# An attention and two MLP layers in one kernel: small VectorE steps on GpSimd, 1/rms stored as rows, an earlier load of the fourth chunk, and 128x128 transposes

## The chip, the cores and the metric

The kernel runs on one core of a Trainium2 chip. A core has TensorE (matrix products and transposes, results in PSUM), VectorE, ScalarE, GpSimd and a queue SP that issues DMAs; all of them run side by side, each works through its own instructions in order, and they wait for each other through semaphores. The metric is the device time of one execution in microseconds (us): 1201.92 us, the median of three runs (1201.45 to 1202.34).

## The reference

```
# q, k, v: [4 batches, 8 heads, 576, 64]
scores = q @ k.T / sqrt(64)
thresh = max(scores, row) - tau                 # tau = 0.02
scores = where(scores >= thresh, scores, -1e9) - max(row)
attn   = exp(scores); attn = attn / (sum(attn, row) + 1e-9)
x      = (attn @ v), heads side by side         # [2304 tokens, 512]

rms = sqrt(mean(x*x, row) + 1e-6)               # first MLP, d_ff 1536
xn  = x / rms * rms_g
x   = (silu(xn @ w_gate) * (xn @ w_val)) @ w_out

h   = x @ w_in                                  # second MLP, d_ff 2048
out = (h * cos(h)) @ w_out2
```

## The kernel before

**Three stages, one stream.** The attention handles 16 pairs of heads (4 batches x 4 pairs). Of each pair, tokens 0 to 511 are four units of 128 rows per head, and the last 64 rows of both heads make a fifth unit (`q4`, `k4`, `v4` hold these rests). The two MLPs work on six chunks of 384 tokens; the first in 6 groups of 2 tiles of d_ff, the second in groups of 3 or 2. In both MLPs every product is three multiplications (`mm3`, L694) of halves: a value is split into a rounded `hi` and a rest `lo`.

**A pair in the attention.** `load_k`, `load_q`, `load_v` issue the DMAs. `prep_pe` transposes q and k on TensorE in three steps a, b, c, and `prep_act` copies them out of PSUM (q scaled by -1/sqrt(64)). The rest of k (64 rows of both heads) is transposed in b and once more in c as a 64-row operand (`k4_t`, L414); the rest of q is scaled by `scale_q4` (VectorE, L417). Then, per unit: `s_mm` (TensorE, L475) makes negated scores for both heads; `s_max` (VectorE, L496) copies them out of PSUM and takes their minimum m; `s_exp` (ScalarE, L514) makes exp(m - s); `s_thr` (VectorE, L505) adds tau to the m of a group of units (two, two, and the last one); `s_mask` (VectorE, L524) multiplies by s <= threshold and sums the row. `t_pe` and `c_pe` transpose the masked exponentials on TensorE, `t_raw` and `c_raw` copy them back, `av` multiplies by v (L599), and `av_out` copies the result. `r_inv` adds 1e-9 to the sums and takes the reciprocal (L533, L534), transposes blocks of 32x32 (L535), `r_out` and `r_in` carry the result through DRAM to one row over all partitions, and `av_div` multiplies (GpSimd, L616). `x_out` stores the pair's x in DRAM.

**The norm.** GpSimd squares and adds the pairs of a batch (`x_sq`, `x_add`), TensorE sums over partitions (`x_sum`), VectorE scales (`x_mean`, L644), GpSimd takes the power -0.5 (`rms`, L648), and two DMAs store 1/rms in DRAM (`rms_out`, L652 and L653): the result lies down the partitions, so each element is stored on its own. A chunk's x is loaded from DRAM, 1/rms of its tokens is loaded to all partitions, GpSimd multiplies, and ScalarE and VectorE split it into `xh` and `xl`.

**What sets the order.** In the attention `Plan` writes the order of all engines: each step has an engine, a cost in ns and a place (`STEPS`), and a greedy loop always takes the step that can start first by these costs; ties go by place. PSUM, loaded tiles and exponentials are counted as buffers. The chunks 0, 1 and 2 and the first four gate-and-value steps of the first MLP (`gv`, TensorE pgv) are in this order too. Behind it stands a plain loop: per step a product with w_out of an earlier step (`o1`, px), the next gate-and-value step, its SiLU and split, and `pump`, which advances weight loads and conversions (up to three at once). In that loop, before the change: the chunks 3 and 4 are loaded ahead of the first turn, chunk 5 two chunks ahead; one chunk ahead GpSimd scales `acc` by 1/rms in one step (L1046) and `split_x` makes the halves (L684, L688). When a chunk's two products with w_out are done, VectorE copies or adds four tiles out of PSUM into `acc` (L1006). The memory of the attention is released before the loop and used again for weights, `acc` and halves.

Of the kernel before, what the change touches and what calls it, by code (L numbers as in the profile page):

```python
# [18 lines left out]
P = 128  # L19
# [9 lines left out]
    "none": ("", 0, 41153),  # L29
    "load_k": ("SP", 1700, -139209, 5000),  # L30
    "load_q": ("SP", 1700, -7544, 7000),
    "load_v": ("SP", 1700, 15881, 5000),
    "q4": ("DVE", 200, -12635),
    "pb": ("PE", 450, -19772),
    "pa": ("PE", 450, -32518),
    "pc": ("PE", 560, -19721),
    "pb_a": ("ACT", 550, 114770),
    "pa_a": ("ACT", 690, -200654),
    "pc_a": ("ACT", 440, -28030),
    "s": ("PE", 1150, -34045),  # L40
    "s4": ("PE", 1050, 22554),
    "warm": ("PE", 640, 119554),
    "max": ("DVE", 830, -156788),
    "exp": ("ACT", 785, 24918),
    "th": ("DVE", 90, 31050),
    "mask": ("DVE", 960, 9378),
    "t": ("PE", 445, 37058),
    "raw": ("ACT", 595, 4406),
    "c0": ("PE", 220, 28723),
    "c1": ("PE", 440, 25563),  # L50
    "c_raw": ("ACT", 415, 126770),
    "rinv": ("DVE", 400, -7759),
    "r_out": ("SP", 2100, 50027, 2500),
    "r_in": ("SP", 1700, 14486, 5000),
    "av0": ("PE", 2300, -173062),
    "av1": ("PE", 2850, -137138),
    "avo": ("ACT", 420, 11229),
    "div": ("POOL", 1420, 191515),
    "xout": ("SP", 500, -109300, 2500),
    "sq": ("POOL", 1200, -50998),  # L60
    "x_add": ("POOL", 1420, 62249),
    "xsum": ("PE", 1150, 65176),
    "mean": ("DVE", 150, -247496),
    "rms": ("POOL", 1330, 44384),
    "rs_out": ("SP", 1000, 78246, 9000),
    "x_load": ("SP", 500, 173724, 6000),
    "x_p": ("POOL", 1000, 66803),
    "x_a": ("ACT", 610, 106078),
    "x_d": ("DVE", 610, 40293),
    "jdma": ("SP", 500, 85880, 5000),  # L70
    "j1": ("DVE", 600, 330),
    "j2": ("DVE", 690, -17065),
    "j_p": ("POOL", 2500, 43119),
    "j_a": ("ACT", 620, 46809),
    "gv": ("PE", 2100, 50075),
    "silu": ("ACT", 500, -103082),
    "hmul": ("DVE", 560, -12918),
    "hhi": ("ACT", 520, 149881),
    "hlo": ("DVE", 720, -101475),
}  # L80
SIGNAL = 100
WARM = (8, 2, 0, 0)
# [10 lines left out]
class Plan:  # L93
# [19 lines left out]
    def order(self):  # L113
# [14 lines left out]
        out = []  # L128
        while len(out) < len(steps):
            best = None  # L130
            for eng, ns in here.items():
                for n in list(ns):
                    s = steps[n]
                    held = [taken[tag][-self.bufs[tag]] for tag, _ in s["take"]
                            if len(taken[tag]) >= self.bufs[tag]]
                    wait = [key for key in held if users.get(key, 1)]
                    if wait:
                        parked.setdefault(wait[0], []).append(n)
                        ns.remove(n)
                        continue  # L140
                    t = max([ready[n], clock[eng]] + [freed[key] for key in held])
                    if best is None or (t, s["place"], n) < best:
                        best = t, s["place"], n
# [3 lines left out]
            eng = s["eng"]  # L147
            here[eng].remove(n)
# [27 lines left out]
def attention_moe_cos_kernel(  # L176
# [27 lines left out]
    IDLE1 = 6  # L204
    G2 = (3, 3, 3, 3, 2, 2)
# [148 lines left out]
    r32 = [acst.tile([P, 32], F32, name=f"r32{i}") for i in range(4)]  # L354
# [58 lines left out]
    def k4_t(ps, p):  # L413
        nc.tensor.transpose(ps, nat["k", p][1].rearrange("p h d -> p (h d)"), ident[:64, :64])  # L414

    def scale_q4(p):
        nc.vector.tensor_scalar(q4[p % 2], q4[p % 2], qscale[:, 0:1], None, op0=ALU.mult)  # L417

    def prep_pe(p, kind):
# [6 lines left out]
        elif kind == "b":  # L426
            k4_t(ps[:, 0:64], p)
            nat_t(ps[:, 64:512], nat["k", p][0], range(3))
        else:
            nat_t(ps, nat["k", p][0], (3,))  # L430
            k4_t(ps[:, 128:192], p)
            nc.tensor.transpose(ps[:, 192:320], q4[p % 2], ident)

    PREP_COLS = {"a": (0, 512), "b": (0, 448), "c": (448, 768)}

    def prep_act(p, kind):
        nm = "q" if kind == "a" else "k"
        if (nm, p) not in qk:
            w = 512 if kind == "a" else S + 192
# [24 lines left out]
    def s_mm(n):  # L464
# [5 lines left out]
        for c in range(2):  # L470
            for hd in heads(n):
                k0 = 288 * c + (0 if hd else 64)
                r = slice(0, P) if u == 4 else slice(64 * hd, 64 * hd + 64)
                lhs = kh[:, S + 64:] if u == 4 else qk["q", p][r, u * P:(u + 1) * P]
# [53 lines left out]

    def r_inv(p):
# [3 lines left out]
        nc.vector.tensor_scalar(r[:, :9], pr[p]["sum"], 1.0e-9, None, op0=ALU.add)  # L533
# [107 lines left out]
    def x_mean(b):  # L641
        ps = sq.pop(("ps", b))
        rm[b] = sm_p.tile([P, 5], F32, tag="rm", name="rm")
        nc.vector.tensor_scalar(rm[b], ps[:, 0:5], 1.0 / DM, 1.0e-6, op0=ALU.mult, op1=ALU.add)  # L644

    def rms(b):

        nc.gpsimd.tensor_tensor(rm[b], rm[b], expo, op=ALU.pow)  # L648

    def rms_out(b):  # L650
        r = rs_dram[b * S:(b + 1) * S]
        nc.sync.dma_start(r[0:512].rearrange("(t p) -> p t", p=P), rm[b][:, 0:4])  # L652
        nc.sync.dma_start(r[512:S], rm[b][64:P, 4:5])  # L653
# [56 lines left out]
    def h_tiles(n):  # L710
        w, t = ((S + 192, "k"), (512, "q"))[n % 2]
# [21 lines left out]
    def gv_h(n):  # L733
        for fn in (h_silu, h_mul, h_hi, h_lo):
            fn(n)

    def attention():
# [84 lines left out]
        for j in range(2 * NPAIRS):  # L822
# [16 lines left out]
            if par:  # L839
                x = add("rinv", n1, r_inv, p, after=[mk[n, hd] for n in range(5 * p, 5 * p + 5) for hd in heads(n)])  # L840
# [8 lines left out]
            if par:  # L849
# [10 lines left out]
                if hp == NP - 1:  # L860
# [4 lines left out]
                    x = add("rms", n1, rms, b, after=[x])  # L865
                    done["rs", b] = add("rs_out", n1, rms_out, b, after=[x])
# [51 lines left out]
        def grow_2():  # L918
            att_s.close()
            late[2] = ctx.enter_context(tc.tile_pool(name="xhl2", bufs=1, side="right"))  # L920

# [19 lines left out]
        )  # L941
        hs = []
# [12 lines left out]
    with tc.manual_schedule():  # L955
# [11 lines left out]
        acc_p = ctx.enter_context(tc.tile_pool(name="acc", bufs=NCH))  # L967
        t_rs = ctx.enter_context(tc.tile_pool(name="rs", bufs=2))
        late.update({c: x_p for c in range(3, NCH)})

# [5 lines left out]

        def load_x(c):
            xrs[c] = t_rs.tile([P, TC], F32, tag="rs", name="rs")
            nc.sync.dma_start(xrs[c], rs_dram[c * TC:(c + 1) * TC].partition_broadcast(P))
            acc[c] = acc_p.tile([P, KD, TC], F32, tag="acc", name="acc")  # L980
            nc.sync.dma_start(acc[c], x_dram[:, :, c * TC:(c + 1) * TC])
# [4 lines left out]
        def o1(n):  # L986
# [13 lines left out]
            if i == fs[-1]:  # L1000
                if c not in acc:
                    acc[c] = acc_p.tile([P, KD, TC], F32, tag="acc", name="acc")
# [22 lines left out]
        load_x(3)  # L1025
        load_x(4)
# [10 lines left out]

        for n in range(N_EARLY, len(seq)):
# [4 lines left out]
            if g == 0 and 4 < c + 2 < NCH and i == fs[0]:  # L1043
                load_x(c + 2)
            if g == 0 and 3 <= c + 1 < NCH and i == fs[0]:
                nc.gpsimd.tensor_tensor(  # L1046
                    acc[c + 1], acc[c + 1],
                    xrs[c + 1][:, None, :].broadcast_to([P, KD, TC]), op=ALU.mult,
                )
# [11 lines left out]
        m1.close()  # L1061

# [143 lines left out]
```

## Time and profile before

| | |
|---|---|
| median of three runs | 1201.92 us |
| the profiled execution, its span | 1201.75 us, 1200.0 us |
| TensorE, busy | 1169.6 us (97%) |
| VectorE, busy | 886.9 us (74%) |
| ScalarE, busy | 648.5 us (54%) |
| GpSimd, busy | 380.1 us (32%) |
| mean granted clock of TensorE | 0.995 of full speed |

The span runs from the first to the last instruction; PE is TensorE's multiplications, PEld its loading of weights, DVE VectorE, ACT ScalarE, POOL GpSimd, SPq the queue of DMA issues. Busy shares are means over stages with different limits, so they are read by stretches: the attention runs to about 334 us, the first MLP to about 770 us, the second to the end.

### The profile page before, as it was taken

The page shows a single profiled execution, that of the slowest core. Times are in us where ns is not written, and L with a number is a line of the kernel's source. Part 1 is how long each engine was busy: PE and PEld are TensorE (multiplying, and loading weights), DVE is VectorE, ACT ScalarE, POOL GpSimd, SP SyncE. Part 2 cuts the span into 40 slices and gives each one's busy share as a digit, 9 for nine tenths or more (in the row PEclk, how much of TensorE's full clock was granted, in tenths as well). Part 3 has the DMA queues.
Part 4 walks back from the last instruction along what each step waited for, and adds up shares of the span by engine and source line. Part 5 has one row for each costly group of instructions (what it writes and reads, how often), then busy time and mean ns, then how long its engine had stood idle before and what let it go on. Part 6 is the DMA issues. An engine that isn't in the chain of part 4 may idle for free.

```text
span 1200.0 us, 18042 instructions
## 1 busy us (share of the span) xinstructions
PE 1169.6 (97%) x6768; PEld 1028.2 (86%) x6768; DVE 886.9 (74%) x1713; ACT 648.5 (54%) x1210; POOL 380.1 (32%) x304
## 2 busy tenths in 40 slices
PE   9999999999969999999999999999999999999997
PEld 7666666666869999999999999999989999999995
DVE  6899989998647864473654737779889798786875
ACT  5777677777524231221312214377677676766663
POOL 0242233422623522040220502214536346252322
PEclk9999999999999999999999999999999999999999
DMA  5433334314341321030110301201202112010014
GB/s 123 119 96 89 96 98 108 75 47 48 110 151 54 91 67 54 1 106 1 53 53 1 98 9 40 67 1 36 70 1 70 36 36 71 1 36 1 1 49 110
DMA packets 99702, 71.11 MB, mean 59 GB/s; under 512 B 65280, under 2 KB 89632, under 8 KB 99616
## 3 DMA queue, kind: packets, MB, share of 16 engines
q1 hardware_dynamic: 99520, 69.94, 21.2%
q8 instruction: 53, 0.87, 0.3%
q14 instruction: 33, 0.27, 0.1%
q0 software_dynamic: 96, 0.03, 0.0%
HBM read 60.43 MB, written 9.52 MB: 58 GB/s over the span
## 4 chain that ended last, share of the span: by engine, by line
PE 83%; DVE 9%; issue 3%; DMA 2%; ACT 1%; POOL 1%; POOLq 0%; SPq 0%; DVEq 0%; ACTq 0%
PE pgv L694 21%; PE ph L694 16%; PE po L694 16%; PE px L694 10%; PE s L475 7%; PE po L599 6%; PE pst L562 4%; DVE e L524 3%; DVE s L496 2%; DMA acc<-x 1%; DMA rs<-rm 1%; PE warm L660 1%; DVE wlo L294 1%; PE psc L581 1%; PE psb L409 1%
## 5 line engine op out<-in xcount | busy, mean ns | idle before, releaser
L283 POOL TENSOR_TENSOR raw<-raw,wtmp 128x512 f32<-128x512 f32 x68 | 101.3, 1490 | 385.8 <-ACT raw L275 252.0
L694 PE MATMUL pgv<-xl,whi 128*128 128x384 f32 x576 | 193.9, 337 | 1.6 <-DVE xl L688 1.6
L694 PE MATMUL pgv<-xh,whi 128*128 128x384 f32 x576 | 194.2, 337 | 0.0
L694 PE MATMUL pgv<-xh,wlo 128*128 128x384 f32 x576 | 193.6, 336 | 0.0
L1111 POOL TENSOR_TENSOR hlo<-r,hhi 128x384 fp32r<-128x384 f32 x96 | 100.5, 1047 | 259.6 <-ACT hhi L1110 239.4
L718 ACT ACTIVATE hh<-pgv 128x384 f32<-128x384 f32 x72 | 35.4, 491 | 234.1 <-PE pgv L694 234.1
L722 DVE TENSOR_TENSOR hh<-hh,pgv 128x384 f32<-128x384 f32 x72 | 39.7, 551 | 140.6 <-ACT hh L718 140.4
L694 PE MATMUL ph<-xh,whi 128*128 128x384 f32 x384 | 129.6, 337 | 0.0
L694 PE MATMUL ph<-xl,whi 128*128 128x384 f32 x384 | 129.5, 337 | 0.0
L694 PE MATMUL ph<-xh,wlo 128*128 128x384 f32 x384 | 129.2, 336 | 0.0
L524 DVE SCALAR_TENSOR_TENSOR e<-s,th,e 128x576 f32<-128x576 f32 x128 | 119.3, 963 | 3.1
L496 DVE TENSOR_SCALAR_CACHE_REDUCE s<-s 128x576 f32<-128x576 f32 x144 | 103.6, 751 | 20.8 <-PE s L475 20.4
L694 PE MATMUL po<-whi,hlo 128*128 128x512 f32 x288 | 114.6, 398 | 1.4 <-POOL hlo L1111 1.4
L1093 ACT ACTIVATE t<-ph,magic 128x384 f32<-128x384 f32 x96 | 55.9, 582 | 110.6 <-PE ph L694 110.6
L694 PE MATMUL po<-whi,hhi 128*128 128x512 f32 x288 | 113.8, 395 | 0.2 <-ACT hhi L1110 0.2
L694 PE MATMUL po<-wlo,hhi 128*128 128x512 f32 x288 | 113.5, 394 | 0.0
L694 PEld LDWEIGHTS pgv<-xl,whi 128*128 128x128 f32 x576 | 108.3, 188 | 2.3 <-DVE xl L688 2.2
L694 PE MATMUL px<-hhi,whi 128*128 128x384 f32 x288 | 99.7, 346 | 10.8 <-ACT raw L275 5.8
L694 PEld LDWEIGHTS pgv<-xh,whi 128*128 128x128 f32 x576 | 108.3, 188 | 0.5 <-issue 0.5
L694 PEld LDWEIGHTS pgv<-xh,wlo 128*128 128x128 f32 x576 | 108.2, 188 | 0.0
L514 ACT ACTIVATE e<-s,m 128x576 f32<-128x576 f32 x128 | 95.4, 781 | 16.3 <-DVE s L496 16.1
L694 PE MATMUL px<-hlo,whi 128*128 128x384 f32 x288 | 99.2, 344 | 0.2
(118 smaller groups left out, 2584.9 us busy)
## 6 DMA issues: line engine op xcount, KB each, us to landing
raw<-in_moe_w_out_dram SPq DMA_DIRECT2D x28, 512.0 KB
raw<-in_moe_w_in_dram SPq DMA_DIRECT2D x16, 512.0 KB
raw<-in_moe_w_gate_dram SPq DMA_DIRECT2D x12, 512.0 KB
raw<-in_moe_w_val_dram SPq DMA_DIRECT2D x12, 512.0 KB
x<-xb SPq DMA_DIRECT2D x16, 288.0 KB
kn<-in_k_dram SPq DMA_DIRECT2D x16, 256.0 KB
qn<-in_q_dram SPq DMA_DIRECT2D x16, 256.0 KB
vn<-in_v_dram SPq DMA_DIRECT2D x16, 256.0 KB
```

The lines of the kernel that those rows point to most:

```text
L283: nc.gpsimd.tensor_tensor(f(lw), f(lw), f(tmp), op=ALU.mult)
L475: nc.tensor.matmul(un[n]["ps", hd][:, c, 0:288], lhs, kh[r, k0:k0 + 288], start=True, stop=True,)
L496: nc.vector.tensor_scalar(s.rearrange("p (c n) -> p c n", c=2), un[n].pop(("ps", hd))[:, :, 0:288], 1.0, None, op0=ALU.mult, op1=ALU.min, ...
L514: nc.scalar.activation(un[n]["e"][:, hd], un[n]["s", hd], AF.Exp, bias=grp[group_of(n)]["m"][:, c], scale=-1.0)
L524: nc.vector.scalar_tensor_tensor(e, un[n].pop(("s", hd)), grp[group_of(n)]["th"][:, ci:ci + 1], e, op0=ALU.is_le, op1=ALU.mult, accum_out= ...
L562: nc.tensor.transpose(ps[:, c], e[:, hd, k0:k0 + P], ident)
L599: nc.tensor.matmul(po[64 * hd:64 * hd + 64, :], vn[:, c, hd, :] if c < 4 else vl[:, hd, :], hf[j]["et"][:, hd, c, :] if c < 4 else hf[j][" ...
L694: nc.tensor.matmul(ps, w[a], x[bb], start=first and i == 0, stop=last and i == 2)
L718: nc.scalar.activation(hq[n], pgv[n][:, 0, 0:TC], AF.Silu)
L722: nc.vector.tensor_tensor(hq[n], hq[n], pgv.pop(n)[:, 1, 0:TC], op=ALU.mult)
L1093: nc.scalar.activation(t, ph, AF.Identity, bias=magic[:, 0:1], scale=INV2PI)
L1111: nc.gpsimd.tensor_tensor(lo, r, f(hi), op=ALU.subtract)
```

## The change

- `scale_q4`, `s_thr` and the addition of 1e-9 (a step of its own now, `r_add`) run on GpSimd in place of VectorE.
- The rest of k is loaded twice, to partitions 0 to 63 and 64 to 127, so that its transposes are 128x128 like all others; the transposed k is 896 columns wide in place of 768, and `s_mm` and `prep_act` use the new columns.
- 1/rms is made in one of six `r32` tiles, transposed in blocks of 32x32 on VectorE (`rms_t`), and stored by five DMAs of rows of 32 elements.
- The fourth chunk (index 3) is loaded and scaled as part of the attention's order, behind the third, into memory of its own (`acc3`). Chunk 4 is loaded, like chunk 5, two chunks ahead in the loop.
- Three calls of `pump` stand before the loop, which start the first three weight loads.
- `Plan` counts 100 ns when a TensorE step has another tiling than the one before; all costs and places in `STEPS` are new.
- A temporary of the second MLP comes from the `hh` pool in place of the `rs` pool, which is closed after the first.

```diff
 STEPS (of the changed lines, those named here)
-    "q4": ("DVE", 200, -12635),
+    "q4": ("POOL", 850, -74898),
-    "pc": ("PE", 560, -19721),
+    "pc": ("PE", 330, -16883),
-    "s": ("PE", 1150, -34045),
+    "s": ("PE", 960, -129359),
-    "th": ("DVE", 90, 31050),
+    "th": ("POOL", 450, -31949),
-    "mask": ("DVE", 960, 9378),
+    "mask": ("DVE", 1040, 10094),
+    "radd": ("POOL", 300, 283),
-    "rs_out": ("SP", 1000, 78246, 9000),
+    "rs_out": ("SP", 2500, -65091, 2500),
-    "x_p": ("POOL", 1000, 66803),
+    "x_p": ("POOL", 1000, 88822),
+SWITCH = 100
+TILING = {"s": 1, "av0": 2, "av1": 2}
...
+                    if eng == "PE" and TILING.get(s["kind"], 0) != tiling:
+                        t = max(t, clock[eng] + SWITCH)
...
-        c = ld_p.tile([64, 2, D], F32, tag="k4", name="k4", bufs=2)
+        c = ld_p.tile([P, 2, D], F32, tag="k4", name="k4", bufs=2)
-        nc.sync.dma_start(c, rest(k, p).rearrange("h p d -> p h d"))
+        for j in range(2):
+            nc.sync.dma_start(c[64 * j:64 * j + 64], rest(k, p).rearrange("h p d -> p h d"))
...
-        nc.tensor.transpose(ps, nat["k", p][1].rearrange("p h d -> p (h d)"), ident[:64, :64])
+        nc.tensor.transpose(ps, nat["k", p][1].rearrange("p h d -> p (h d)"), ident)
...
-        nc.vector.tensor_scalar(q4[p % 2], q4[p % 2], qscale[:, 0:1], None, op0=ALU.mult)
+        nc.gpsimd.tensor_scalar(q4[p % 2], q4[p % 2], qscale[:, 0:1], None, op0=ALU.mult)
...
-        nc.vector.tensor_scalar(th[:, :w], grp[g]["m"][:, :w], tau_c[:, 0:1], None, op0=ALU.add)
+        nc.gpsimd.tensor_scalar(th[:, :w], grp[g]["m"][:, :w], tau_c[:, 0:1], None, op0=ALU.add)
...
+    def r_add(p):
+        nc.gpsimd.tensor_scalar(r32[p % 4][:, :9], pr[p]["sum"], 1.0e-9, None, op0=ALU.add)
...
-        rm[b] = sm_p.tile([P, 5], F32, tag="rm", name="rm")
+        rm[b] = r32[4 + b % 2]
...
+    def rms_t(b):
+        rt = sm_p.tile([P, 32], F32, tag="rt", name="rt", bufs=4)
+        nc.vector.transpose(rt, rm[b])
+        rm[b] = rt
...
-        nc.sync.dma_start(r[0:512].rearrange("(t p) -> p t", p=P), rm[b][:, 0:4])
-        nc.sync.dma_start(r[512:S], rm[b][64:P, 4:5])
+        dst = rs_dram[b * S:b * S + 512].rearrange("(t b i) -> b t i", b=4, i=32)
+        for i in range(4):
+            nc.sync.dma_start(dst[i], rm[b][32 * i:32 * i + 4, :])
+        nc.sync.dma_start(
+            rs_dram[b * S + 512:(b + 1) * S].rearrange("(b i) -> b i", i=32), rm[b][68::32, :]
+        )
...
+        x = add("x_load", NU + 6, load_x, 3, after=[g2, done["rs", 2]] + x0 + [done[x] for x in range(8, 12)])
+        add("x_p", NU + 6, scale_x, 3, after=[x])
...
-        load_x(3)
-        load_x(4)
...
+        for _ in range(3):
+            pump(3)
...
-            if g == 0 and 4 < c + 2 < NCH and i == fs[0]:
+            if g == 0 and 4 <= c + 2 < NCH and i == fs[0]:
                 load_x(c + 2)
```

## Rows read from the trace of the kernel before

**Rows 1.** The page's busy time, share of the span and instructions of each engine.
```profile
PE 1169.6 (97%) x6768; PEld 1028.2 (86%) x6768; DVE 886.9 (74%) x1713; ACT 648.5 (54%) x1210; POOL 380.1 (32%) x304
```

**Rows 2.** Busy time by stretches: length, PE, PEld, DVE, ACT, POOL (instructions), clock, DMA.
```profile
30.00:300.00 270.00, 262.16 (x1877) 176.49 (x1876) 247.83 (x644) 203.74 (x371) 79.98 (x57) 1.00 0.36 86
334.00:366.00 32.00, 21.67 (x104) 21.06 (x103) 14.36 (x23) 5.19 (x11) 8.78 (x5) 0.84 0.42 142
```

**Rows 3.** Chain of waits, 334 to 404 us: start, duration, what.
```profile
334.54 9.67 DMA rs<-rm
...
344.36 4.76 DMA acc<-x
...
365.27 4.33 PE pgv L694 x24
...
397.51 2.12 PE px L694 x12
399.63 4.16 PE pgv L694 x24
```

**Rows 4.** TensorE's timeline: start, duration; in brackets the idle time before, its releaser.
```profile
334.32 0.34 PE L694 MATMUL pgv<-xh,whi 128*128 128x384 f32 x1
...
345.23 0.69 PE L694 MATMUL px<-hhi,whi 128*128 128x384 f32 x1 [4.50 <-DVE acc L1006]
...
361.09 0.66 PE L694 MATMUL px<-hhi,whi 128*128 128x384 f32 x1 [5.82 <-ACT raw L275]
```

**Rows 5.** VectorE's timeline, 344 to 378 us.
```profile
344.62 1.95 DVE L1006 COPY acc<-px 128x384 f32<-128x384 f32 x4 [3.66 <-DMA rs<-rm]
353.47 5.41 DVE L688 SCALAR_TENSOR_TENSOR xl<-acc,g_sb,xh 128x384 fp32r<-128x384 f32 x4 [6.90 <-ACT xh L684]
...
360.40 1.94 DVE L1006 COPY acc<-px 128x384 f32<-128x384 f32 x4
...
375.34 2.19 DVE L688 SCALAR_TENSOR_TENSOR xl<-acc,g_sb,xh 128x384 fp32r<-128x384 f32 x4
```

**Rows 6.** GpSimd: groups to 420 us (busy, mean ns, idle before), one timeline row.
```profile
L1046 POOL TENSOR_TENSOR acc<-acc,rs 128x1536 f32<-128x1536 f32 x3 | 10.9, 3645 | 15.8 <-DMA acc<-x 15.8
L681 POOL TENSOR_TENSOR xe<-xe 128x384 f32<-128x384 f32 x8 | 8.7, 1111 | 0.0
L648 POOL TENSOR_TENSOR rm<-rm,expo 128x5 f32<-128x5 f32 x4 | 6.6, 1646 | 3.0 <-DVE rm L644 3.0
...
325.37 4.24 POOL L681 TENSOR_TENSOR xe<-xe 128x384 f32<-128x384 f32 x4
```

**Rows 7.** Issues on SP's queue, timeline: the start, and the last pair's sums.
```profile
1.58 0.68 SPq L397 DMA_DIRECT2D k<-in_k_dram  x1
...
313.07 1.36 SPq L542 DMA_DIRECT2D rd<-rt  x4
315.31 0.45 SPq L548 DMA_DIRECT2D rb<-rd  x1
```

**Rows 8.** TensorE's timeline: a third preparation step, and twenty transposes in a row.
```profile
214.70 0.33 PE L409 MATMUL psc<-ident,kn 128*128 128x128 f32 x1
...
215.32 0.60 PE L562 MATMUL pst<-ident,el 128*128 128x128 f32 x4
...
238.13 2.42 PE L562 MATMUL pst<-ident,e 128*128 128x128 f32 x20
```

**Rows 9.** VectorE's small steps, groups from 24 to 305 us.
```profile
L505 DVE TENSOR_SCALAR th<-m,tau_c 128x4 f32<-128x4 f32 (+1 forms) x45 | 12.5, 278 | 0.3
L533 DVE TENSOR_SCALAR r<-sum 128x9 f32<-128x9 f32 x15 | 5.0, 332 | 0.4
L417 DVE TENSOR_SCALAR q<-q,qscale 128x128 f32<-128x128 f32 x14 | 4.8, 343 | 0.0
```

**Rows 10.** The masks (L524): ns min/median/max, and their busy time from 30 to 300 us.
```profile
L524 DVE SCALAR_TENSOR_TENSOR e<-s,th,e x128: 805/816/2035, 13.6 to 308.1; 128x576 f32<-128x576 f32 x128
...
30.00:300.00 270.00, 118.75 (x257) 1.00 0.36 86
```

More of the change, by code (lines that the diff above doesn't have):

```diff
@@ L128, in order @@
         out = []
+        tiling = 0
         while len(out) < len(steps):
@@ L204, in attention_moe_cos_kernel @@
     IDLE1 = 6
+    KW = 896
     G2 = (3, 3, 3, 3, 2, 2)
@@ L353, in attention_moe_cos_kernel @@
     nat, qk, un, hf, pr, xb, rm, sq, pre = {}, {}, {}, {}, {}, {}, {}, {}, {}
-    r32 = [acst.tile([P, 32], F32, name=f"r32{i}") for i in range(4)]
+    r32 = [acst.tile([P, 32], F32, name=f"r32{i}") for i in range(6)]
     for t in q4 + v4 + r32:
@@ L735, in gv_h, with acc_tile, load_x, scale_x @@
             fn(n)
+    def acc_tile(c, shape):
+        return late["acc", c].tile(shape, F32, tag="acc", name="acc")
+    def load_x(c):
+        xrs[c] = late["rs", c].tile([P, TC], F32, tag="rs", name="rs")
+        nc.sync.dma_start(xrs[c], rs_dram[c * TC:(c + 1) * TC].partition_broadcast(P))
+        acc[c] = acc_tile(c, [P, KD, TC])
+        nc.sync.dma_start(acc[c], x_dram[:, :, c * TC:(c + 1) * TC])
+    def scale_x(c):
+        nc.gpsimd.tensor_tensor(
+            acc[c], acc[c], xrs[c][:, None, :].broadcast_to([P, KD, TC]), op=ALU.mult
+        )
     def attention():
@@ L839, in attention @@
             if par:
-                x = add("rinv", n1, r_inv, p, after=[mk[n, hd] for n in range(5 * p, 5 * p + 5) for hd in heads(n)])
+                x = add("radd", n1, r_add, p, after=[mk[n, hd] for n in range(5 * p, 5 * p + 5) for hd in heads(n)])
+                x = add("rinv", n1, r_inv, p, after=[x])
                 x = add("r_out", n1, r_out, p, after=[x])
@@ L865, in attention @@
                     x = add("rms", n1, rms, b, after=[x])
+                    x = add("mean", n1, rms_t, b, after=[x])
                     done["rs", b] = add("rs_out", n1, rms_out, b, after=[x])
@@ L920, in grow_2 @@
             late[2] = ctx.enter_context(tc.tile_pool(name="xhl2", bufs=1, side="right"))
+            late["acc", 3] = ctx.enter_context(tc.tile_pool(name="acc3", bufs=1, side="right"))
+            late["rs", 3] = ss_p
         ends = [mk[n, hd] for n in range(NU - 10, NU) for hd in heads(n)]
@@ L1001, in o1 @@
                 if c not in acc:
-                    acc[c] = acc_p.tile([P, KD, TC], F32, tag="acc", name="acc")
+                    acc[c] = acc_tile(c, [P, KD, TC])
                 for d in range(KD):
@@ L1091, in reduce2 @@
             ph, r = pend[n]
-            t = t_rs.tile([P, TC], F32, tag="rs", name="t")
+            t = late["hh"].tile([P, TC], F32, tag="hh", name="t")
             nc.scalar.activation(t, ph, AF.Identity, bias=magic[:, 0:1], scale=INV2PI)
@@ L1144, in o2 @@
                 if g == g1:
-                    acc[c] = acc_p.tile([P, NTT, DM], F32, tag="acc", name="acc")
+                    acc[c] = acc_tile(c, [P, NTT, DM])
                 for t in range(NTT):
```

136 lines of the change are left out of this document (67 added, 69 removed).

## The prediction

> **What bounds the kernel now.** I read the busy table first: TensorE is busy for 97% of the span, VectorE for 74%, GpSimd for 32% [rows 1]. An average says little here, so the second view was the busy time by stretches [rows 2]. From 30 to 300 us (the attention) TensorE is busy for 262.16 of 270 us and VectorE for 247.83: TensorE sets the pace with 7.84 us of holes, VectorE follows with only 22 us free, and GpSimd has 190 us free. From 334 to 366 us (the change-over to the first MLP) TensorE is busy for only 21.67 of 32 us, at a mean granted clock of 0.84, a mix of its two levels (1.2 and 2.4 GHz). So there are two places to win: a thin margin spread over the attention, and one hole of some 14 us.
>
> The chain of waits over that hole [rows 3] begins with 9.67 us for the write of 1/rms (rs<-rm) and 4.76 us for a load of x. TensorE's timeline [rows 4] shows its two stops: 4.50 us before 345.23 and 5.82 us before 361.09. The first is ended by VectorE's copy out of PSUM, which itself stood until the write of rs had finished [rows 5]; rs and the copy have no data in common, so I read it as memory that rm held and acc took over. The second is named as a wait for ScalarE, but that multiplication (px) reads nothing of raw. VectorE's rows explain it: the four xl of the fourth chunk began at 353.47 after a wait of 6.90 us, ran for 5.41 us, and the copies that free PSUM for px came behind them at 360.40. The root is the late fourth chunk.
>
> **The change part by part.** The sum is made against the profiled execution's own 1201.75 us (span 1200.0), 0.17 us under the median of the three timed runs.
>
> *A. The hole.* From the first pgv multiplication at 334.32 to the one that follows the second stop at 365.27 pass 30.95 us [rows 3, 4]. The work in between is two gate-and-value steps and four px steps; undisturbed these take 4.16 and 2.12 us [rows 3], together 16.80. The excess is 14.15 us: the two stops, and behind each of them multiplications at the low clock. After the change the fourth chunk needs only batch 2, whose rs was written long before; its two loads are issued behind those of the third chunk, and its scaling stands in the attention's order. GpSimd is done with the third chunk at 329.6 (325.37 + 4.24 [rows 6]); one more step on 128x1536, 3.645 us by its mean, ends at about 333.3, before the first gate-and-value and px steps are over (334.32 + 4.16 + 2.12 = 340.6), which is when the fourth chunk is split. The copy loses its cause as well: rm moves to a tile that isn't released to acc, and the rows that replace it are written by five stores, like the four of rd<-rt. Those took 1.36 us to issue, and the load that needs them was issued 0.88 us after that [rows 7]; so about 2.6 us in place of 9.67. What is late next: px still has to wait for the first of four copies, as from 360.40 to 361.09, 0.7 us, twice. So 14.15 - 1.4 = **12.75 us**. The fifth chunk's load moves behind the first three weight loads on SP's queue; its split comes 24.5 us after the first pgv (3 x 4.16 + 5 x 2.12 + 1.4), time enough for a load and a scaling. Those weight loads now start before the loop, ahead of the steps that use them by as much as before. Bounds: 5 (only the first stop goes) to 14.15.
>
> *B. Transposes of 128x128.* In the third preparation step three transposes, one of them 64x64, take 0.62 us until the next transpose can start (214.70 to 215.32) [rows 8]. Twenty 128x128 transposes take 2.42 us, 0.113 each after the first, so three would be 0.34: 0.28 us saved. The first preparation step has such a 64x64 one too, behind scores that use half the rows as well; I count nothing for it. Sixteen pairs: 16 x 0.28 = **4.5 us**, directly on the engine that sets the pace. Bounds: 0 (the stretch is VectorE's just then) to 9 (both steps). The 64 more columns that ScalarE copies hide behind its free quarter (203.74 of 270 us busy [rows 2]). The second load of k's rest costs one more issue per pair on SP, 0.68 us [rows 7], which has slack but at the start: there q's load comes 0.7 us later, **-0.7** (0 to -1.4).
>
> *C. VectorE's small steps.* From 24 to 305 us the thresholds take VectorE 12.5 us, the sums 5.0, the scaling of q4 4.8 [rows 9]: 22.3 us go, and four block transposes of a few tens of columns come. Since TensorE sets the pace, relief of VectorE can pay no more than TensorE's holes, 7.84 us, and some 1 us in the tail, where masks are on the path. I take half of the holes, **3.9 us**. On GpSimd nothing of this form is in the trace. A line through its 128x384 (1.111) and 128x1536 (3.645) gives 0.27 us plus 2.2 ns per column [rows 6], an estimate of 0.28 us for a threshold or a sum and 0.55 for q4: 64 x 0.28 + 16 x 0.55 = 27 us in all, on an engine with 190 free. The other end is the nearest row in size, the power on 128x5, 1.646 us. I take the line, since the power is the one step there that is not plain arithmetic. Behind a threshold stand the masks of its group in VectorE's order, and another GpSimd step may be ahead of it. The exponentials of ScalarE, which the mask needs too, cover part of that wait, and VectorE's 44 us (22 free, 22 freed) the rest.
>
> VectorE's steps are stretched beside GpSimd's: the four xl took 5.41 us beside the scaling of the next chunk and 2.19 later [rows 5], and a mask takes 0.816 us at the median and 2.035 at worst [rows 10]. The Trainium skill (SBUF — State Buffer, section "SBUF: two separate sides") says that VectorE and GpSimd share one pair of ports as an exclusive lock for a whole instruction, and counts VectorE steps with two SBUF inputs among the takers. The trace agrees, and by that rule part of this relief is taken back; that is the first rival.
>
> *D. Order and tail.* All places of the order are new, and it now counts 100 ns for a change of TensorE's tiling. The 0.28 us above are two changes, 0.14 each; three fewer a pair would give 16 x 3 x 0.14 = 6.7 us, but scores and the products with v already stand side by side often. I take 0 (0 to 6.7). GpSimd's 3.6 us for the fourth chunk are a step of 1 us in the order's costs; it may stand ahead of the power or of the third chunk: **-0.5** (0 to -3.6).
>
> Sum: 12.75 + 4.5 + 3.9 - 0.7 - 0.5 = 19.95, so 1201.75 - 19.95 = **1181.8 us**.
>
> **The rivals.**
> 1. *The shared port takes the relief back.* Masks fill 118.75 of 270 us [rows 10], 44%, so of 27 us of new GpSimd work 12 fall on a mask; with the queueing behind long steps nothing is left of C, at worst -3. 1201.75 - 12.75 - 4.5 + 1.2 = 1185.7, to 1188.7. For it: the stretched rows. Against: only a GpSimd step that meets a mask costs, and 27 us is short beside 190 free.
> 2. *The second stop stays*, because the fourth chunk's xl are again stretched beside the fifth's scaling, or its load comes late. It costs 5.82 - 0.7 = 5.1: 1186.9. Against: seven us of room.
> 3. *Slower: VectorE stops at the thresholds.* If one takes 1.65 us on GpSimd as the power does, and VectorE stands meanwhile, 48 x (1.65 - 0.28) = 66 us of stops (0.28 by the line is taken as covered) meet 44 free ones; 22 us lengthen the attention and C is lost: 1181.8 + 3.9 + 22 = 1207.7. It decides from (44 + 16) / 48 = 1.25 us of stop per threshold, where 16 is A and B less the two small costs. Against: it needs the odd row to be the rule.
> 4. *More.* VectorE held up more of the attention than TensorE's holes show: the other 3.9 of the holes, 1 of the tail, and 6.7 of the order: 1181.8 - 11.6 = 1170.2. For it: VectorE is busy for 92% of that stage.
>
> **How the numbers follow.** Forecast 0.52 (own range 1177 to 1186), rival 1 0.18, rival 2 0.08, rival 3 0.08, rival 4 0.14. The range of 1168 to 1194 holds all but rival 3 and the outer ends of the others. 0.2% (2.4 us) is about what a measurement can tell from no change. Faster: forecast, rivals 2 and 4, and all but 0.03 of rival 1, 0.89; within 0.2%: that 0.03, where the port eats into A and B too; slower: rival 3, 0.08.
>
> **What would show it.** A: no wait of VectorE for rs, TensorE with stops under 1 us and the granted clock at its upper level throughout the change-over. B: three psc transposes in about 0.35 us. C: threshold rows on GpSimd near 0.3 us, VectorE's busy time in the attention down by 15 us or more; masks with a mean that rises as this time falls would be rival 1, waits of VectorE for GpSimd of over 1 us at the thresholds rival 3. I am wrong if the attention's end comes no earlier than before, or if another wait stands in the change-over.

## The result and the profile after

The changed kernel takes **1188.95 us** (median of 4 runs, 1188.72 to 1189.27) against 1201.68 us beside it on the same chip: a ratio of 0.9895, 95% interval 0.9878 to 0.9912. It is faster by 12.7 us. I had said 1181.8 us with a range of 1168 to 1194: the sign and the range hold, but 7 of the 20 us are missing. The profiled execution took 1189.27 us, its span is 1187.0 us.

First the busy table of the changed kernel, then its busy time by stretches (columns as in [rows 2]; 320 to 340 us is an extra stretch):

```profile
PE 1161.9 (98%) x6768; PEld 1024.4 (86%) x6768; DVE 859.2 (72%) x1639; ACT 647.8 (55%) x1210; POOL 431.4 (36%) x384
```

```profile
30.00:300.00 270.00, 263.33 (x1919) 179.82 (x1918) 233.40 (x595) 209.40 (x381) 129.34 (x129) 1.00 0.34 91
334.00:366.00 32.00, 29.06 (x157) 28.02 (x156) 23.96 (x37) 11.64 (x22) 15.36 (x8) 0.96 0.44 138
320.00:340.00 20.00, 17.02 (x84) 16.31 (x83) 10.91 (x16) 7.20 (x15) 8.03 (x5) 0.83 0.42 128
```

Against [rows 2], VectorE's time in the attention fell by 14.4 us and GpSimd's rose by 49.4. TensorE's busy share hardly moved, but in the same 270 us it now runs 1919 multiplications in place of 1877: the attention got faster though the share of busy time says nothing of it. From 334 to 366 us the hole has nearly closed (21.67 us busy became 29.06). The third row shows where a new one opened: 320 to 340 us, at a mean granted clock of 0.83.

The milestones say how much each stage gave. The fifth gate-and-value step, the first behind the attention's own (first pgv at 334.32 in [rows 4]), starts at 325.79: 8.5 us earlier. The seventh started at 365.07 before and starts at 350.74 now, so from the fifth to the seventh there were 30.75 us and now are 24.95: 5.8 us. The six steps behind that take 42.4 us in place of 40.7: 1.7 us are given back. From there to the end the two kernels are equal to 0.4 us.

TensorE's timeline of the changed kernel around the new hole (columns as in [rows 4]):

```profile
325.79 0.34 PE L717 MATMUL pgv<-xh,whi 128*128 128x384 f32 x1
...
327.35 0.34 PE L717 MATMUL pgv<-xh,whi 128*128 128x384 f32 x1
330.57 0.69 PE L717 MATMUL pgv<-xl,whi 128*128 128x384 f32 x1 [2.88 <-DVE xl L711]
331.05 0.52 PE L717 MATMUL pgv<-xh,wlo 128*128 128x384 f32 x1
...
336.49 0.44 PE L717 MATMUL px<-hlo,whi 128*128 128x384 f32 x1
...
348.57 0.42 PE L717 MATMUL px<-hhi,whi 128*128 128x384 f32 x1 [1.72 <-DVE acc L1046]
...
350.74 0.34 PE L717 MATMUL pgv<-xh,whi 128*128 128x384 f32 x1
```

The stop of 2.88 us is a wait for one xl tile. Behind it 17 multiplications start in 5.44 us, 0.32 apart in place of the 0.173 that they need elsewhere. The granted clock from 331.05 to 336.2 us is 0.50, the lower of its two levels (1.2 GHz); with the first of them some 2.8 us are lost. VectorE's and GpSimd's timelines say why the tile was late, first VectorE's:

```profile
325.03 1.67 DVE L711 SCALAR_TENSOR_TENSOR xl<-xe,g_sb,xh 128x384 fp32r<-128x384 f32 x3
326.73 0.21 DVE L667 STREAM_TRANSPOSE rt<-r 128x32 f32<-128x32 f32 x1
326.86 3.65 DVE L711 SCALAR_TENSOR_TENSOR xl<-xe,g_sb,xh 128x384 fp32r<-128x384 f32 x1
336.04 0.56 DVE L745 TENSOR_TENSOR hh<-hh,pgv 128x384 f32<-128x384 f32 x1 [5.52 <-ACT hh L741]
...
337.64 1.95 DVE L1046 COPY acc<-px 128x384 f32<-128x384 f32 x4
```

```profile
325.19 1.50 POOL L662 TENSOR_TENSOR r<-r,expo 128x5 f32<-128x5 f32 x1 [2.07 <-DVE r L656]
326.67 3.43 POOL L770 TENSOR_TENSOR acc<-acc,rs 128x1536 f32<-128x1536 f32 x1
```

Three of the third chunk's xl took 1.67 us together. Then VectorE turned to the block transposition of 1/rms, which needs GpSimd's power; while it did, GpSimd went from the power to the scaling of the fourth chunk. The last xl began 0.19 us behind that scaling and took 3.65 us, until 0.41 us after the scaling (326.67 + 3.43 = 330.10) was over. The Trainium skill (SBUF — State Buffer, section "SBUF: two separate sides") says that the first to start keeps the shared ports for its whole instruction. The rows of the scaling agree. The row of the power does not: by it the power ran from 325.19 to 326.69 us, and beside it two of the three xl began and ended at their usual 0.61 us. The prediction, which named that rule, applied it to the masks and to another chunk's xl, not to this one.

The copy out of PSUM that waited for rs in [rows 5] now starts right behind VectorE's own work. SP's issues of the changed kernel (columns as in [rows 7]) show the five stores and the load that needs them:

```profile
326.96 1.27 SPq L673 DMA_DIRECT2D rs<-rt  x4
328.28 0.50 SPq L674 DMA_DIRECT2D rs<-rt  x1
...
332.30 0.35 SPq L765 DMA_DIRECT2D rs<-rs  x1
```

Last GpSimd's groups from 24 to 305 us (columns as in [rows 6]), the third preparation step of one pair on TensorE, and for the masks their durations (ns min/median/max) and what VectorE stood for ahead of them:

```profile
L515 POOL TENSOR_SCALAR th<-m,tau_c 128x4 f32<-128x4 f32 (+1 forms) x45 | 31.9, 709 | 87.9 <-DVE s L506 87.9
...
L427 POOL TENSOR_SCALAR q<-q,qscale 128x128 f32<-128x128 f32 x13 | 10.6, 816 | 1.0 <-DMA q<-in_q_dram 0.9
...
L540 POOL TENSOR_SCALAR r<-sum 128x9 f32<-128x9 f32 x16 | 7.1, 443 | 40.6 <-DVE el L534 40.3
```

```profile
217.97 0.31 PE L419 MATMUL psc<-ident,kn 128*128 128x128 f32 x1
218.12 0.27 PE L424 MATMUL psc<-ident,k 128*128 128x128 f32 x1
218.23 0.27 PE L442 MATMUL psc<-ident,q 128*128 128x128 f32 x1
218.44 1.24 PE L485 MATMUL s<-k,q 64*128 64x288 f32 x8
```

```profile
L534 DVE SCALAR_TENSOR_TENSOR e<-s,th,e x128: 775/815/1960, 13.6 to 298.6; 128x576 f32<-128x576 f32 x128
...
  POOL th L515: 1.5, 5
```

A threshold takes 0.71 us on GpSimd, 2.5 times my estimate, and yet VectorE stood for thresholds only 1.5 us in all, and the masks are no slower than in [rows 10]. The three transposes follow each other by 0.15 and 0.11 us, and the scores behind them start 0.47 us after the first; with the 64x64 one among them it was 0.62 to the next step [rows 8].

### The profile page after: what moved, and what is told of

It is laid out like the page before. It is cut to its first block, busy times and chain, and to the rows that moved or that the text cites. A ratio compares the mean times of both kernels' runs of the same rounds, so it can differ in the third digit from the quotient of the medians.

```text
span 1187.0 us, 18156 instructions
## 1 busy us (share of the span) xinstructions
PE 1161.9 (98%) x6768; PEld 1024.4 (86%) x6768; DVE 859.2 (72%) x1639; ACT 647.8 (55%) x1210; POOL 431.4 (36%) x384
## 4 chain that ended last, share of the span: by engine, by line
PE 83%; DVE 8%; issue 4%; ACT 2%; POOL 1%; DMA 1%; SPq 0%; POOLq 0%; ACTq 0%; DVEq 0%
PE pgv L717 21%; PE ph L717 16%; PE po L717 16%; PE px L717 11%; PE s L485 6%; PE po L611 5%; PE pst L574 4%; DVE e L534 2%; DVE s L506 1%; DVE wlo L303 1%; DVE xl L711 1%; PE psc L593 1%; DVE raw L286 1%; ACT et L584 1%; PE psa L419 1%
## 5 line engine op out<-in xcount | busy, mean ns | idle before, releaser
L524 ACT ACTIVATE e<-s,m 128x576 f32<-128x576 f32 x128 | 96.0, 783 | 9.0 <-DVE s L506 8.6
```

The source lines that it names most:

```text
L524: nc.scalar.activation(un[n]["e"][:, hd], un[n]["s", hd], AF.Exp, bias=grp[group_of(n)]["m"][:, c], scale=-1.0)
```

## The experiments

Each kernel below is the changed one with one edit, or with two where that is said, timed beside the kernel before. Where nothing else is said, the order in which the steps are written out is the changed kernel's. The end of the attention is taken as the start of the fifth gate-and-value step (325.79 us in the changed kernel). One profile each stands behind such a start, and it varies: with the stored columns (9) it is 2.0 us later, with the later product (10), an edit behind the attention, 1.7. In both some 1.6 us are lost at the same place: from 90.8 to 93.2 us, behind a wait of 1.16 us, TensorE's granted clock is 0.50, where it is 1.00 in the changed kernel with as much idle time there. So a difference of less than 2 us between two starts is no finding.

**1. The small steps back on VectorE.**

```diff
-        nc.gpsimd.tensor_scalar(th[:, :w], grp[g]["m"][:, :w], ...)    # and q4, and the sums
+        nc.vector.tensor_scalar(th[:, :w], grp[g]["m"][:, :w], ...)
```

> The changed kernel with the thresholds, the sums and the scaling of q4 back on VectorE, at the same places of the same order. Theory (the relief of VectorE pays about half of TensorE's holes): 3 to 5 us slower than the changed kernel's 1188.95, so 1192 to 1194, VectorE's busy time from 30 to 300 us up by some 15 us from 233. Rival (TensorE sets the pace, and what GpSimd's new steps take from VectorE through the shared port equals what they give): within 1 us, 1188 to 1190. A faster time would mean that the move itself cost.

Measured: 1196.46 us (1195.14 to 1197.5), ratio 0.9956, interval 0.9944 to 0.9967. The attention ends at 335.58, 9.8 us later than in the changed kernel and 1.3 later than before. TensorE's timeline at that start, what TensorE waited for in the scores from 30 to 300 us (engine, what waited, for what: us in total, times, longest us), and the attention's stretch of this kernel:

```profile
335.58 0.34 PE L717 MATMUL pgv<-xh,whi 128*128 128x384 f32 x1
```

```profile
PE s L485 <- DVE s L506: 7.1, 8, 1.4
```

```profile
30.00:300.00 270.00, 258.27 (x1855) 174.48 (x1854) 243.03 (x643) 202.35 (x368) 80.50 (x57) 0.99 0.33 86
```

TensorE does 64 multiplications fewer in the same time than in the changed kernel. The relief of VectorE is worth 7.5 us of the whole in this order, twice what I had taken for it. The 9.8 us at the end of the attention look like more than the 7.84 us of holes that I took for a bound, but those are the holes of the kernel before. Without the relief the new order has 270 - 258.27 = 11.73 us of holes in the same stretch, and the changed kernel 6.67. What relief can pay is read against the holes of the order that it stands in; that VectorE holds up more than TensorE's holes show, as my fourth rival had it, is not shown.

**2. The rest of k transposed 64x64 again.**

```diff
-        nc.tensor.transpose(ps, nat["k", p][1].rearrange("p h d -> p (h d)"), ident)
+        nc.tensor.transpose(ps, nat["k", p][1].rearrange("p h d -> p (h d)"), ident[:64, :64])
```

The single load and the 768 columns come back with it.

> The changed kernel with the 64x64 transposes of k's rest as they were before (one load, 64 rows, 768 columns of transposed k), at the same places of the same order. Theory (each third preparation step loses 0.28 us of TensorE's own time): 16 x 0.28 = 4.5 us slower, 1193.5, with 0.62 us from the first psc transpose to the next step instead of some 0.35. Rival (in these stretches VectorE sets the pace, so TensorE's time is free): within 1 us of 1188.95.

Measured: 1191.7 us (1191.5 to 1192.08), ratio 0.9917, interval 0.9904 to 0.993. The attention ends at 330.24, 4.45 us later, close to the 4.5 us of term B:

```profile
330.24 0.34 PE L716 MATMUL pgv<-xh,whi 128*128 128x384 f32 x1
```

The first scores begin at 7.51 us here and at 8.16 in the changed kernel, which loads the rest of k twice. So the 4.45 are the transposes' 5.1 less 0.65 for the second load. By the medians 2.75 us arrive at the end. Most of the rest comes back in the change-over by the clock: the same stop of 2.88 us stands there, but 9 multiplications at the lower clock follow it in place of 17, and the fifth to the seventh step take 23.70 us in place of 24.95.

**3. Both undone together.** The edits of 1 and 2 in one kernel.

> Two parts undone together, in the changed kernel's order: thresholds, sums and q4 on VectorE, and the rest of k loaded once and transposed 64x64. Alone, the first brought the fifth gate-and-value step (the end of the attention) to 335.6 us, the second to 330.2; the changed kernel has it at 325.8. Theory: with the small steps on VectorE it is VectorE that sets the pace of the attention, so TensorE's 4.5 us per 16 pairs are hidden: the step comes within 1.5 us of 335.6, and the time is 1196 to 1198. Rival: the two add up, since TensorE sets the pace in both: the step comes at about 340, and the time is 1199.5 to 1202.

Measured: 1199.04 us (1196.92 to 1201.89), ratio 0.9968, interval 0.9957 to 0.9979; the attention ends at 337.22, 1.6 us later than with the first edit alone, where 4.45 would add up to 340. TensorE's timeline at that start and the attention's stretch:

```profile
337.22 0.34 PE L716 MATMUL pgv<-xh,whi 128*128 128x384 f32 x1
```

```profile
30.00:300.00 270.00, 260.20 (x1840) 172.85 (x1838) 241.46 (x638) 200.08 (x365) 81.06 (x57) 0.99 0.32 84
```

This does not decide between the two. The start lies just past the theory's end and the time between the two expectations. The trace speaks for the theory: TensorE's holes are 9.80 us in place of 11.73, so part of the longer transposes went into them. The medians speak for the rival: 1199.04 is 2.58 us above experiment 1, as 1191.7 is 2.75 above the changed kernel. Whether B and C are independent in this order stays open; experiment 5 has more on it.

**4. The costs and places of before, steps on GpSimd.** The order is made as if the small steps were still VectorE's, at their costs of before; the instructions themselves go to GpSimd.

```diff
-    "th": ("POOL", 450, -31949),
+    "th": ("DVE", 90, 31050),       # and all other costs and places of before
-    "radd": ("POOL", 300, 283),
+    "radd": ("DVE", 0, -7759),
-SWITCH = 100
+SWITCH = 0
```

> The changed kernel with the order that follows from the costs and places of the kernel before, without the 100 ns for a change of tiling; all steps run on the engines of the changed kernel. Theory (of the 8.5 us that the stretch up to the fifth gate-and-value step gained, some 4 come from the new order): 3 to 6 us slower, 1192 to 1195. Rival (the order is worth nothing, as the prediction took it): within 1 us of 1188.95, but for the stop at the third chunk's xl, which may move by its own 5 us; the trace then shows the same time up to that step.

Measured: 1211.23 us (1208.39 to 1215.62), ratio 1.0082, interval 1.0063 to 1.0101: slower than before, and 22 us slower than the same instructions in the new order. VectorE's waits from 30 to 300 us, then TensorE's, then the stretch:

```profile
DVE e L534 <- POOL th L515: 18.3, 21, 2.9
DVE r L546 <- POOL r L540: 5.1, 12, 1.0
DVE el L534 <- POOL th L515: 4.8, 2, 2.5
```

```profile
PE s L485 <- DVE s L506: 15.5, 12, 2.9
```

```profile
30.00:300.00 270.00, 250.74 (x1763) 169.87 (x1763) 217.34 (x542) 192.90 (x349) 104.90 (x120) 0.97 0.33 86
```

This is the mechanism of my third rival, in another order: VectorE stands for thresholds 23.1 us, up to 2.9 us at once. My theory, an order worth 4 us, fell by 18.

**5. The costs and places of before, steps on VectorE.** The same order, with the instructions of the small steps on VectorE too.

> The order that follows from the costs and places of the kernel before, with the thresholds, the sums and q4's scaling on VectorE as before: of the change the 128x128 transposes, the rows of 1/rms, the fourth chunk's load and the early weight loads are left. Theory (without the new order the small steps belong on VectorE; the rest of the change is worth 4.5 us of transposes and some 4 us of the change-over by itself): 1192 to 1195, far below the 1211.23 of the same order with these steps on GpSimd. Rival (the old costs and places are bad for the new program whichever engine has the small steps): above 1200.

Measured: 1195.01 us (1194.37 to 1197.72), ratio 0.9946, interval 0.9933 to 0.9959: the time as expected, but not by its parts. TensorE's timeline at the end of the attention, then the attention's stretch:

```profile
335.47 0.34 PE L717 MATMUL pgv<-xh,whi 128*128 128x384 f32 x1
```

```profile
30.00:300.00 270.00, 256.59 (x1863) 174.32 (x1863) 246.68 (x639) 202.57 (x367) 81.04 (x57) 1.00 0.33 88
```

The attention ends at 335.47, 1.1 us later than before, though its transposes are 128x128; TensorE's holes are 13.41 us in place of 7.84. So of the 4.5 us of transposes nothing arrived: in this order, with the small steps on VectorE, the time that TensorE saved became holes. The gain is the change-over's, 21.70 us from the fifth to the seventh step in place of 30.75. With 1 and 4 this completes a square: old order 1195.0 on VectorE and 1211.2 on GpSimd, new order 1196.5 and 1188.95. In the old order the move costs 16 us, in the new one it gives 7.5; neither the move nor the order gives anything alone.

**6. The transposition of 1/rms behind the third chunk's xl.** Only VectorE's order changes (`rms_t` and the row stores are emitted behind the fourth xl).

```diff
-        plan.run()
+        plan.run(norm, x2)      # norm: rms_t and rs_out of the last batch; x2: the third chunk
```

> The changed kernel with one VectorE step moved: the block transpose of the last batch's 1/rms (and the stores of it) stands behind the fourth xl of the third chunk in place of ahead of it. The scaling of pss stays early, since the run before showed that px waits for its PSUM bank. Theory (port lock): the fourth xl starts at about 326.6, some 0.05 us before GpSimd's scaling of the fourth chunk, and takes 0.6 us in place of 3.65; the stop at pgv falls under 0.5 us and the low clock after it goes, 4 to 5 us faster than 1188.95, so 1184 to 1185. Rival 1 (GpSimd takes the port first): the xl is stretched as before, 1188 to 1189.5. Rival 2 (the time is given back between 340 and 385 us, where px and pgv wait for copies and xl): 1186.5 to 1188.

Measured: 1184.06 us (1183.98 to 1185.61), ratio 0.9853, interval 0.984 to 0.9865: 4.9 us faster than the changed kernel. VectorE's and GpSimd's timelines, then TensorE's stops to 352 us and the stretch from 320 to 340 us:

```profile
325.12 2.19 DVE L725 SCALAR_TENSOR_TENSOR xl<-xe,g_sb,xh 128x384 fp32r<-128x384 f32 x4
327.23 0.20 DVE L681 STREAM_TRANSPOSE rt<-r 128x32 f32<-128x32 f32 x1
```

```profile
326.76 3.92 POOL L784 TENSOR_TENSOR acc<-acc,rs 128x1536 f32<-128x1536 f32 x1
```

```profile
333.06 0.44 PE L731 MATMUL px<-hhi,whi 128*128 128x384 f32 x1 [0.76 <-DVE acc L1061]
...
343.38 0.41 PE L731 MATMUL px<-hhi,whi 128*128 128x384 f32 x1 [1.72 <-DVE acc L1061]
```

```profile
320.00:340.00 20.00, 19.24 (x115) 18.85 (x114) 10.84 (x22) 7.98 (x16) 8.61 (x5) 1.00 0.48 146
```

The fourth xl starts at 326.70, 0.06 us ahead of GpSimd's scaling. The four xl run in 2.19 us, the scaling is the one that is held (3.92 us in place of 3.43), and nobody waits for it. The stop of 2.88 us and the low clock are gone; the two waits for copies stay.

**7. The whole norm behind the xl.** As 6, but `x_mean`, the power and the scaling too; this one ran ahead of 6.

> The changed kernel with VectorE's two steps of the last batch's norm (the scaling and the block transpose) moved behind the four xl of the third chunk, and nothing else moved: GpSimd's power, and with it its scaling of the fourth chunk, can then start only when those xl are done. Theory (the stop of 2.88 us before 330.57 is the last xl, 3.65 us long, held at the shared port by GpSimd's 3.43 us of scaling, and the low clock after it costs 2.4 us more): the stop goes, 5.3 us faster, 1183.7. Rival 1 (the stop belongs to something else, so a wait of over 2 us stands at the same pgv): 1188 to 1190. Rival 2 (the time comes back in the conversion of weights between 360 and 385 us): 1186 to 1189 with longer waits for xl and copies there.

Measured: 1187.68 us (1186.5 to 1189.21), ratio 0.9885, interval 0.9871 to 0.9899. The xl took 2.21 us, but TensorE got another stop:

```profile
327.27 0.44 PE L731 MATMUL px<-hhi,whi 128*128 128x384 f32 x1 [1.93 <-DVE r L670]
```

The product with w_out needs the PSUM that `x_mean` reads, and `x_mean` now stood behind the xl. Most of the gain of 6 is lost to it; the step to move was the transposition alone.

**8. The fourth chunk in the loop again.**

```diff
-        x = add("x_load", NU + 6, load_x, 3, after=[...])
-        add("x_p", NU + 6, scale_x, 3, after=[x])
...
+        load_x(3)
```

> The changed kernel with the fourth chunk's load and scaling back ahead of the loop's first steps, outside the attention's order; rows of 1/rms and the early weight loads stay. Theory A (the hole was the late fourth chunk): the load is issued when rs has been stored, at about 330, lands at 335, is scaled by 339; then the four xl wait and px with them, one stop of 2 to 4 us and some low clock, but no collision with the third chunk's xl (which gives 5 back): 1187 to 1190. Theory B (the stored rows alone closed the hole): 1184 to 1186, faster than the changed kernel. Rival (the full hole returns): 1196 to 1199.

Measured: 1190.73 us (1187.13 to 1190.91), ratio 0.9897, interval 0.9883 to 0.9911: not to be told from the changed kernel. The last xl of the third chunk takes 0.58 us here, as GpSimd has no scaling to do then; the stop comes later, when the fourth chunk is late (TensorE's timeline, then VectorE's):

```profile
346.44 0.41 PE L717 MATMUL px<-hhi,whi 128*128 128x384 f32 x1 [4.69 <-DVE acc L1044]
```

```profile
339.68 2.21 DVE L711 SCALAR_TENSOR_TENSOR xl<-acc,g_sb,xh 128x384 fp32r<-128x384 f32 x4 [5.19 <-ACT xh L707]
```

So as it was placed the early load took away one stop and made another of about the same price. Against 6, where it does no harm, the fourth chunk's early load is worth 6.7 us by the medians. The profiled execution above was the fastest of the five (1187.13), and against that one it is 3.1; my price for the second stop, 5.1, lies between.

**9. 1/rms by columns again**, in all four batches and without the transposition; the fourth chunk stays early.

```diff
-        rm[b] = r32[4 + b % 2]
+        rm[b] = sm_p.tile([P, 5], F32, tag="rm", name="rm")
...
+        nc.sync.dma_start(r[0:512].rearrange("(t p) -> p t", p=P), rm[b][:, 0:4])
```

> 1/rms is stored by columns again (two DMAs from a tile of the small pool that is released to the first MLP), without the block transposition; the fourth chunk stays in the attention's order and all other places stay. Theory: with the fourth chunk early the write of 1/rms of the last batch has nothing behind it that is due: the power ends at about 326.7, 9.7 us of writing end at about 336.4, and the first copy into acc was due at 337.6 anyway; the fifth chunk is scaled only at 353. And the transposition no longer stands between the third and the fourth xl of the third chunk, so the fourth begins before GpSimd's scaling does: 1184 to 1187 us, no stop of over 1 us before the gate-and-value product at 330. Rival: the stored rows are what removes the copy's wait; then VectorE's copy waits for rs again by 2 us or more, TensorE stops at the product with w_out behind it, and the time is 1190 to 1194.

Measured: 1192.71 us (1191.54 to 1194.58), ratio 0.9926, interval 0.9913 to 0.994. The theory fell, the rival holds (VectorE's timeline, then TensorE's):

```profile
339.22 1.95 DVE L1041 COPY acc<-px 128x384 f32<-128x384 f32 x4 [4.78 <-DMA rs<-rm]
```

```profile
339.83 0.69 PE L712 MATMUL px<-hhi,whi 128*128 128x384 f32 x1 [5.62 <-DVE acc L1041]
```

The four xl ran undisturbed (2.19 us), as expected, but that made the first copy due some 5 us earlier (as in 6), and the write of the columns, 9.75 us in the chain of waits, was not done. I had taken the due time from the kernel with the stop. Against 6, the stored rows are worth 8.7 us by the medians; of that the profiles show 6.3 in the change-over (25.96 us from the fifth to the seventh step in place of 19.65), and 1.9 are this profile's late attention.

**10. The product with w_out behind the gate-and-value product**, on top of 6: in the loop the second product of a turn is issued between `gv_mm` and `gv_h`, so that the copies have more time.

```diff
-            if done < n - 1:
+            if done < n - 1 and n == N_EARLY:
                 next_o1()
...
+            if done < n - 1 and n > N_EARLY:
+                next_o1()
```

> The kernel of the run with the transpose moved, and in the loop's second and third step the extra product with w_out (px) behind the gate-and-value multiplications in place of ahead of them, so that 4 us of multiplications lie between a chunk's last px and the px that needs its PSUM banks. Theory (px waits for copies that nothing covers: stops of about 0.4 to 0.8 and 1.7 us): 2.5 us faster than that run, 1181.5 to 1183. Rival (the two stops come back as waits of pgv for xl of the fourth chunk, or in the weight conversions): within 1 us of that run.

Measured: 1182.96 us (1181.95 to 1183.53), ratio 0.9839, interval 0.9827 to 0.9852: the fastest version, faster than both kernels. TensorE has no marked stop between 325 and 355 us any more; a new one of 1.38 us for an xl ends at 358.97:

```profile
355.10 0.41 PE L731 MATMUL px<-hhi,whi 128*128 128x384 f32 x1 [0.32 <-DVE acc L1061]
358.97 0.45 PE L731 MATMUL pgv<-xl,whi 128*128 128x384 f32 x1 [1.38 <-DVE xl L725]
```

It gains 1.1 us on 6 where I had expected 2.5. In the profiled execution the rest is lost in the attention, not in the loop: from the fifth to the thirteenth gate-and-value step it takes 59.94 us, and 6 takes 62.10, so the loop gave 2.2 us, and the late attention spoken of above took 1.6 of them. How often the other runs lost that is not known.

## Why the prediction was right and where it was wrong

**The time.** The measured 1188.95 us lies in the stated range, but 3 us outside the forecast's own (1177 to 1186), and it stands beside the first rival's 1185.7 to 1188.7, whose cause the runs do not show. A alone came out 7 us short; what was given back later and what the attention gave beyond its forecast nearly cancel.

**A, the hole (12.75 us forecast, 5.8 measured).** This is the step that failed. Both stops of [rows 4] went, for the reasons given: stored rows freed the copy (experiment 9), the early fourth chunk freed the second product (experiment 8). What I missed is the step "one more step on 128x1536 ... ends at about 333.3, before the first gate-and-value and px steps are over". It ended at 330.1, earlier still, and that was the harm: it ran while VectorE split the third chunk. I asked only whether the result would be in time, not what the 3.6 us would hold up. In D I priced the same step as a delay on GpSimd's own queue (0.5 us, at most 3.6), when its price was a stop of 2.88 us on TensorE and 2.8 us of low clock behind it; experiment 6 gives 4.9 us back by moving a transposition of 0.2 us, and its 19.65 us from the fifth to the seventh step are 11.1 fewer than before, most of what A promised. The waits for the first copies, put at 0.7 us twice, came to some 0.3 and 1.72.

One sentence of A is wrong outright: what is stored is the transposed tile, and that one comes from the same small pool as rm before, whose memory is released to the first MLP as well. The copy does not wait because the five stores are over in time; with columns stored from that pool it waits again (experiment 9). And 365.27 is not where the step behind the second stop starts; that is 365.07, so the excess was 13.95 us. The three weight loads ahead of the loop were not tested by themselves.

**B, transposes (4.5 us).** 4.45 us at the attention's end in the changed kernel, or 5.1 without the second load's 0.65 (experiment 2). The prediction added B and C as if they were independent. In the order of before, with the small steps on VectorE, nothing of B arrived (experiment 5); in the new order experiment 3 leaves it open (1.6 us at the attention's end, 2.58 of the whole).

**The start (-0.7).** The first scores begin at 8.16 us, before the change at 8.22, as if the later load had cost nothing. With one load, in the same order, they begin at 7.51 (experiment 2): the later load cost 0.65 us, as priced, and the rest of the change made up for it.

**C and D, relief and order (3.9 and 0 us).** Together with B and the start I forecast 7.7 us for the attention and 8.5 came; less the 4.45 of B and the start, relief and order together gave some 4, close to the 3.9 of C. That is in part luck, since the parts were not what I took them for. The thresholds took 0.71 us, the sums 0.44 and q4 0.82, in place of 0.28, 0.28 and 0.55. That VectorE did not stand for them is the order's doing: experiment 4 shows the same steps, placed as VectorE's, costing 16 us more than on VectorE. "I take 0" for the order held only for the order by itself (1195.0 and 1196.5 us with the small steps on VectorE); with the move it decides between 16 us lost and 7.5 gained.

**The rivals.** The first (the port eats the relief): refuted for the masks, whose mean is 947 ns (963 before); the port took its share on GpSimd's side of the attention, by the lengthened small steps, and in the change-over. That last point was in no rival: the second had it for the fourth chunk's xl, a chunk too late. The third is refuted for this order and real for another. The fourth is not borne out: the time is 19 us above its own, and its mechanism is not shown (experiment 1).

**What was given back.** From the seventh to the thirteenth gate-and-value step the changed kernel is 1.7 us slower; its stops of 1.12, 0.92, 0.78 and 0.52 us (behind xl and xh, beside GpSimd's conversions of weights) stand against 0.42, 1.05 and 0.53 before. The attention, the small steps and the stored rows have no part in it: experiments 1 to 7 and 9 all take 42.4 to 42.5 us for these six steps. With the fourth chunk in the loop (8) it is 41.4. I tried nothing else on these.

## What to carry to other kernels

When a step is moved earlier onto an engine with time to spare, ask not only whether its result is in time but which instruction of the neighbour begins while it runs: here an early 3.4 us step on GpSimd cost about as much as the late one, and moving a 0.2 us step undid it. A move of small steps to another engine and the order around it can be one change: here the order alone made the kernel no faster, and the move alone made it much slower. And a due time read in a trace with a stop in it holds only as long as the stop does.

## What the runs showed of the hardware

- One xl on 128x384 took 0.58 us alone and 3.65 us when it began 0.19 us behind a GpSimd step of 3.43 us; begun 0.06 us first, VectorE's was whole (four in 2.19 us) and GpSimd's took 3.92. Beside GpSimd's power on 128x5 (1.50 us by its row) two xl kept their 0.61 us.
- A threshold on 128x4 took 294 ns at the least on GpSimd, as a line through the long steps had it, but 709 on the mean. VectorE holds it up: in the changed kernel's trace 38 of the 48 thresholds (all sizes) began while VectorE ran a step with two SBUF inputs (a mask, an xl, a conversion of weights), took 604 to 1069 ns, and 36 of them ended 160 to 177 ns behind that step; the other 10 took 294 to 427.
- After a stop of 2.88 us TensorE ran 17 multiplications at the lower clock (granted clock 0.50), in experiment 2 after an equal stop 9; without the stop (6) the granted clock from 320 to 340 us was 1.00.
